# One x tile, not two, through the PE transposes at the start of a gated attention and FFN kernel

## The chip, the cores and the metric

The kernel runs on one core of one Trainium2 chip. The metric is the device time of one execution in microseconds (us), lower is better. PE is the matmul engine (TensorE), PEld its weight loads, DVE is VectorE, ACT is ScalarE, SP is the engine that issues most DMAs, and "SPq" and "ACTq" are the queues on which a DMA is issued.

## The reference, cut to what matters

Two blocks share one input `x` of 2048 tokens by 512 features, in bf16: a linear attention and a gated feed-forward network, mixed by a gate per token.

```python
g = sigmoid((x * gate_w).sum(-1, keepdims=True))
q, k, v = split(x @ wqkv)                 # 32 heads of 16
pq, pk = phi(q), phi(k)                   # phi(t) = (t + 1 if t > 0 else exp(t)) + 1e-6
kv = einsum("bhsd,bhse->bhde", pk, v); z = pk.sum(over tokens)
a = ((pq @ kv) / (pq @ z + 1e-6)) @ wo
b = (silu(x @ w1) * (x @ w3)) @ w2
return g * a + (1 - g) * b
```

## The kernel before

The kernel cuts the tokens into 16 tiles of 128. It needs `x` twice: feature-major (`xT`), as the weights of every matmul that contracts over features, and token-major (`x_sb`), for `XP`, the sum over tokens of `x` times `pk`, from which it gets `kv` later. Tiles 0 and 1 are loaded token-major first and transposed by PE, because those transposes can start before anything else is there. The other tiles come transposed by DMA, and their token-major copies by plain loads later on the same queue.

```python
TF = 2
x_first = x2d[0 : TF * P, :].rearrange("(p j) d -> p j d", j=TF)
dq.dma_start(out=x_sb[:, 0:TF, :], in_=x_first)                      # tiles 0, 1: 256 KB, on SP
nc.scalar.dma_start(out=wk_sb[:, 0:2, :], in_=wqkv_r[:, 0:2, D : 2 * D])   # on ACT
dq.dma_start(out=wk_sb[:, 2:4, :], in_=wqkv_r[:, 2:4, D : 2 * D])
...
dq.dma_start(out=xT[:, :, TF * P : TB], in_=x2d[TF * P : TB, :], transpose=True)   # tiles 2, 3
for tb in range(1, NTB):                                             # four tiles each
    dq.dma_start(out=xT[:, :, tb * TB : (tb + 1) * TB],
                 in_=x2d[tb * TB : (tb + 1) * TB, :], transpose=True)
    x_ts = slice(TF if tb == 1 else tb * TPB, (tb + 1) * TPB)
    dq.dma_start(out=x_sb[:, x_ts, :], in_=x_r[:, x_ts, :])
...  # the other weights follow on the same queue

emit_warm(TB, TB, TB, TB, TB, TB, P, P, P)   # matmuls on constants: keep PE busy until x is there
...
emit_xT(0)                                   # PE transposes, then one copy each on DVE and ACT
emit_xT(1)
for kc, t in ((0, 0), (1, 0), (0, 1), (1, 1), (2, 0), (3, 0)):
    emit_k_mm(k0[t], t, kc)
...  # the rest of k of tiles 0 to 3
for t in range(TPB, NT):                     # from tile 4 on: XP of an earlier tile, then k of tile t
    for u in range(n_xp, n_xp + (2 if t == NT - 4 else 1)):
        emit_xp(u, XP_ps)                    # XP of tile u: needs x_sb of tile u and pk of tile u
        n_xp = u + 1
    emit_k(t)
```

In the timeline below PE runs in the order in which the code emits: XP of tile 0, k of tile 4, XP of tile 1, k of tile 5, and so on.

## Time and profile before

| | before |
|---|---|
| time, median of 3 runs | 179.96 us (179.65 to 180.22) |
| span of the profiled execution | 177.7 us |
| PE busy | 173.0 us, 97% of the span |
| the chain that ended last | 97% PE |

The chain of the page (its part 4) follows the last instruction back to whatever released it, step by step. It is PE almost from end to end, so time can be won or lost only where PE is made to do less, to start earlier or to wait. From the page of the kernel before:

```profile
span 177.7 us, 2453 instructions
PE 173.0 (97%) x868; PEld 83.8 (47%) x884; DVE 117.8 (66%) x203; ACT 65.9 (37%) x124; POOL 63.2 (36%) x71
PE 97%; issue 1%; DVE 0%; DVEq 0%
```

The timeline of the kernel before gives start, length, engine, source line, operation, output and inputs, and the number of merged instructions; a selection of the lines of PE and of the SP queue in the first 12 us:

```profile
0.84 3.04 PE L163 MATMUL warm<-const-bfloat16-1.0 128*128 128x512 bf16 x9 [0.84 <-PEq L473]
1.73 1.32 SPq L89 DMA_TRANSPOSE xT<-in_A_x_dram  x1
3.10 2.81 SPq L93 DMA_TRANSPOSE xT<-in_A_x_dram  x1
3.92 0.89 PE L176 MATMUL xTp<-ident,x_sb 128*128 128x128 bf16 x8
4.70 3.63 PE L186 MATMUL k<-wk_sb,xT 128*128 128x512 bf16 x16
5.96 0.58 SPq L98 DMA_DIRECT2D x_sb<-in_A_x_dram  x1
8.17 1.03 PE L206 MATMUL XP<-pk_sb,x_sb 128*128 128x512 bf16 x4
9.03 1.03 PE L186 MATMUL k_ps<-wk_sb,xT 128*128 128x512 bf16 x4
9.89 1.03 PE L206 MATMUL XP<-pk_sb,x_sb 128*128 128x512 bf16 x4
10.76 1.03 PE L186 MATMUL k_ps<-wk_sb,xT 128*128 128x512 bf16 x4
```

XP of tile 1 is the line at 9.89. PE has no visible gap in these merged lines; the waits view has one wait of 0.3 us, of the first transpose for x. A line on SPq is the time that the issue holds the queue; the data land later. The DMA view of issues that started in a short window gives each landing (the last column is us from issue to landing). For the kernel before, windows around the transposes of tiles 2-3 and 4-7 and the x_sb load behind them:

```profile
xT<-in_A_x_dram SPq DMA_TRANSPOSE x1, 4.5
xT<-in_A_x_dram SPq DMA_TRANSPOSE x1, 4.9
x_sb<-in_A_x_dram SPq DMA_DIRECT2D x1, 768.0 KB, 5.0
```

With the issue times above, tiles 2-3 land at 1.73 + 4.5 = 6.2 us, tiles 4-7 at 8.0, and the token-major tiles 2-7 at 11.0.

### The profile page before, as it was taken

Reading aid. Unit: us, or ns where it says so; the run is one execution under the profiler, and the core shown is the slowest. Engines: PE = TensorE matmul, PEld = TensorE weight load, DVE = VectorE, ACT = ScalarE, POOL = GpSimd, SP = SyncE. Lnnn points to the kernel's source line nnn. Section 1 sums busy time; section 2 is a strip of 40 time slices with the busy share of each in tenths; the row PEclk is TensorE's granted clock in tenths of the full one; section 3 lists DMA queues with packets and bytes.
Section 4 is the critical chain, followed back from the end, with each engine's and each line's share of the span. In section 5 each row is a group of like instructions: output and inputs, shape, how many; then the busy total and the mean of one; then the engine's idle time right before and its main releaser. Section 6 shows DMA issues by size and latency. Waiting matters only on the chain.

```text
span 177.7 us, 2453 instructions
## 1 busy us (share of the span) xinstructions
PE 173.0 (97%) x868; PEld 83.8 (47%) x884; DVE 117.8 (66%) x203; ACT 65.9 (37%) x124; POOL 63.2 (36%) x71
## 2 busy tenths in 40 slices
PE   8999999999999999999999999999999999999993
PEld 3444444474445444444454544444545444444463
DVE  0596858898998637597776466878754668775000
ACT  3624224466433333333244333243434323241211
POOL 5197655967262323262003232710032328000000
PEclk9999999999999999999999999999999999999999
DMA  5999999911014011124000111230002022200011
GB/s 175 234 291 248 300 306 365 348 46 28 9 30 90 6 42 36 38 59 89 0 4 7 40 33 37 71 78 6 0 7 66 7 70 59 59 0 0 30 45 48
DMA packets 30252, 15.14 MB, mean 85 GB/s; under 512 B 20672, under 2 KB 30112, under 8 KB 30240
## 3 DMA queue, kind: packets, MB, share of 16 engines
q1 hardware_dynamic: 29968, 14.72, 30.6%
q10 hardware_dynamic: 272, 0.26, 0.5%
q8 instruction: 7, 0.11, 0.3%
q14 instruction: 5, 0.04, 0.1%
HBM read 8.42 MB, written 2.10 MB: 59 GB/s over the span
## 4 chain that ended last, share of the span: by engine, by line
PE 97%; issue 1%; DVE 0%; DVEq 0%
PE o_ps L357 19%; PE up_ps L320 19%; PE gate_ps L312 19%; PE o_ps L348 8%; PE XP L206 8%; PE q_ps L219 8%; PE k_ps L186 6%; PE r_ps L243 3%; PE k L186 2%; PE o_ps L352 2%; PE warm L163 2%; PE kvT_ps L418 1%; PE xTp L176 0%; PE W_ps L440 0%; PE z_ps L431 0%
## 5 line engine op out<-in xcount | busy, mean ns | idle before, releaser
L312 PE MATMUL gate_ps<-xT,w_sb 128*128 128x512 bf16 x157 | 40.8, 379 | 0.1
L320 PE MATMUL up_ps<-xT,w_sb 128*128 128x512 bf16 x157 | 40.6, 379 | 0.2
L227 POOL TENSOR_TENSOR qz<-pq,z_sb 128x512 f32<-128x512 bf16 x16 | 18.5, 1162 | 59.7 <-DVE pq L147 58.4
L325 ACT ACTIVATE th<-gate_ps 128x512 bf16<-128x512 f32 x40 | 23.9, 597 | 37.9 <-PE gate_ps L312 36.4
L357 PE MATMUL o_ps<-w_sb,hT 128*128 128x512 bf16 (+2 forms) x177 | 37.4, 355 | 0.2
L327 DVE SCALAR_TENSOR_TENSOR gs<-th,gate_ps 128x512 bf16<-128x512 bf16 x40 | 27.3, 682 | 5.6 <-ACT th L325 5.3
L330 DVE TENSOR_TENSOR hT<-up_ps,gs 128x512 bf16<-128x512 f32 x40 | 27.6, 691 | 3.7
L144 DVE TENSOR_SCALAR phi_m<-phi_e 128x512 bf16<-128x512 bf16 x32 | 14.1, 441 | 21.3 <-ACT phi_e L142 21.2
L357 PEld LDWEIGHTS <-hT 128*128 128x128 bf16 x180 | 16.8, 97 | 17.9
L320 PEld LDWEIGHTS <-w_sb 128*128 128x128 bf16 x160 | 15.6, 98 | 18.9
L312 PEld LDWEIGHTS <-w_sb 128*128 128x128 bf16 x160 | 15.6, 98 | 18.7
L362 ACT ACTIVATE o_out<-o_ps,omg 128x512 bf16<-128x512 f32 (+2 forms) x17 | 11.1, 656 | 30.4 <-PE o_ps L357 30.4
L292 POOL TENSOR_TENSOR pqn<-pq,rden 128x512 bf16<-128x512 bf16 x16 | 16.6, 1055 | 14.0 <-DVE rden L285 11.7
L196 POOL TENSOR_TENSOR pks<-pks,pk_sb 128x512 f32<-128x512 f32 x15 | 17.4, 1161 | 7.3 <-DVE pk_sb L147 6.7
L348 PE MATMUL o_ps<-W_sb,pqT 128*128 128x512 bf16 (+2 forms) x70 | 16.7, 355 | 0.1
L230 DVE TENSOR_REDUCE den<-qz 128x32 f32<-128x512 f32 x16 | 10.9, 684 | 8.6 <-POOL qz L227 8.5
L206 PE MATMUL XP<-pk_sb,x_sb 128*128 128x512 bf16 x62 | 16.2, 379 | 0.1
L219 PE MATMUL q_ps<-wq_sb,xT 128*128 128x512 bf16 x61 | 16.1, 380 | 0.1
L142 ACT ACTIVATE phi_e<-k_ps 128x512 bf16<-128x512 f32 x12 | 7.2, 597 | 14.4 <-PE k_ps L186 14.4
L142 ACT ACTIVATE phi_e<-q_ps 128x512 bf16<-128x512 f32 x16 | 9.6, 597 | 7.8 <-PE q_ps L219 6.7
L186 PE MATMUL k_ps<-wk_sb,xT 128*128 128x512 bf16 x48 | 12.3, 379 | 0.0
L147 DVE SCALAR_TENSOR_TENSOR pq<-q_ps,phi_m 128x512 bf16<-128x512 f32 x16 | 11.1, 691 | 0.5
(59 smaller groups left out, 117.3 us busy)
## 6 DMA issues: line engine op xcount, KB each, us to landing
w_sb<-in_B_w_dram SPq DMA_DIRECT2D x6, 640.0 KB, 9.1
out_dram<-o_out SPq DMA_DIRECT2D x15, 128.0 KB, 1.9
x_sb<-in_A_x_dram SPq DMA_DIRECT2D x2, 512.0 KB, 4.2
x_sb<-in_A_x_dram SPq DMA_DIRECT2D x1, 768.0 KB, 5.0
wq_sb<-in_A_wqkv_dram SPq DMA_DIRECT2D x1, 512.0 KB, 5.0
wv_sb<-in_A_wqkv_dram SPq DMA_DIRECT2D x1, 512.0 KB, 6.5
wo_sb<-in_A_wo_dram SPq DMA_DIRECT2D x1, 512.0 KB, 10.4
wk_sb<-in_A_wqkv_dram ACTq DMA_DIRECT2D x1, 256.0 KB, 3.6
```

What stands on the lines that cost most here:

```text
L186: nc.tensor.matmul(k_ps[:], lhsT=xT[:, kc, t * P : (t + 1) * P], rhs=wk_sb[:, kc, :], start=(kc == 0), stop=(kc == KC - 1),)
L196: nc.gpsimd.tensor_add(pks[:], pks[:], pk_sb[:, t, :])
L206: nc.tensor.matmul(XP_ps[dc][:], lhsT=x_sb[:, t, dc * P : (dc + 1) * P], rhs=pk_sb[:, t, :], start=(t == 0), stop=(t == NT - 1),)
L219: nc.tensor.matmul(q_ps[:], lhsT=xT[:, kc, ts_tok], rhs=wq_sb[:, kc, :], start=(kc == 0), stop=(kc == KC - 1),)
L227: nc.gpsimd.tensor_tensor(out=qz[:], in0=st[tb, "pq"][:, tt, :], in1=z_sb[:], op=ALU.mult)
L312: nc.tensor.matmul(gate_ps[:], lhsT=w1_sb[:, kc, fsl], rhs=xT[:, kc, tok_sl], start=(kc == 0), stop=(kc == KC - 1),)
L320: nc.tensor.matmul(up_ps[:], lhsT=w3_sb[:, kc, fsl], rhs=xT[:, kc, tok_sl], start=(kc == 0), stop=(kc == KC - 1),)
L325: nc.scalar.activation(out=th[:], in_=gate_ps[:], func=ACT.Tanh, scale=0.5)
L327: nc.vector.scalar_tensor_tensor(out=gs[:], in0=th[:], scalar=1.0, in1=gate_ps[:], op0=ALU.add, op1=ALU.mult)
L330: nc.vector.tensor_tensor(out=st[tb, "hT"][:, fc, :], in0=up_ps[:], in1=gs[:], op=ALU.mult)
L348: nc.tensor.matmul(o_ps[:], lhsT=st[tb, "pqT"][:, c, tsl], rhs=W_sb[:, c, a:b], start=(c == 0), stop=False,)
L357: nc.tensor.matmul(o_ps[:], lhsT=st[tb, "hT"][:, fc, tsl], rhs=w2_sb[:, fc, a:b], start=False, stop=(fc == FC - 1),)
```

## The change

The intent: only tile 0 goes through PE, so the first load is half as large, PE transposes half as much and k can start earlier. Tile 1 now comes transposed by its own small DMA, behind `wk`, and its token-major copy comes with those of tiles 2 and 3, behind the transpose of tiles 4-7. The cut diff:

```diff
-    TF = 2
-    x_first = x2d[0 : TF * P, :].rearrange("(p j) d -> p j d", j=TF)
-    dq.dma_start(out=x_sb[:, 0:TF, :], in_=x_first)
+    dq.dma_start(out=x_sb[:, 0, :], in_=x_r[:, 0, :])
 ...
-    dq.dma_start(
-        out=xT[:, :, TF * P : TB], in_=x2d[TF * P : TB, :], transpose=True
-    )
+    for a, b in ((P, 2 * P), (2 * P, TB)):
+        dq.dma_start(out=xT[:, :, a:b], in_=x2d[a:b, :], transpose=True)
     for tb in range(1, NTB):
         ...  # the transpose of four tiles
-        x_ts = slice(TF if tb == 1 else tb * TPB, (tb + 1) * TPB)
-        dq.dma_start(out=x_sb[:, x_ts, :], in_=x_r[:, x_ts, :])
+        if tb == 1:
+            dq.dma_start(out=x_sb[:, 1:TPB, :], in_=x_r[:, 1:TPB, :])
+        if tb < NTB - 1:
+            x_ts = slice(tb * TPB, NT if tb == NTB - 2 else (tb + 1) * TPB)
+            dq.dma_start(out=x_sb[:, x_ts, :], in_=x_r[:, x_ts, :])
 ...  # w2 in one load in place of two; outputs of tiles 0 and 1 in plain rows
-    emit_warm(TB, TB, TB, TB, TB, TB, P, P, P)
+    emit_warm(TB, TB, TB, TB, TB, P, P)
 ...
     emit_xT(0)
-    emit_xT(1)
-    ...  # k of tiles 0 and 1 interleaved
+    emit_warm(TB)
+    ...  # k of tiles 0 to 3 in order
```

## The prediction

> **What bounds the kernel.** TensorE. On the page of before PE is busy 173.0 of 177.7 us (97%), and the chain that ended last is 97% PE. In the timeline PE runs without a visible gap from 0.84 us: nine warm-ups to 3.88, eight transposes 3.92 to 4.81, k of tiles 0-3 to 8.33, then XP and k in turn, 0.86 us each. So only what shortens or delays PE in the first 12 us can move the time. Weights have slack: wq lands at 20.7 us (first used at 29.9), the first w1 half at about 27 (used at 38.2).
>
> **What the change does.**
> - Removes four PE transposes (eight took 0.89 us, so about 0.45) and their two copies.
> - One 512-wide warm-up (0.43 us start to start) and one 128-wide fewer before the transposes, one 512-wide behind them, to cover the copy.
> - x tile 0 is 128 KB in place of 256 KB. The 256 KB landed at 3.91 us and PE waited 0.3 us for it (waits view). At 300 to 340 GB/s half should land near 3.3.
> - Tile 1 (128 rows) becomes a DMA transpose. From 4.5 to 7.4 us the first two transposes moved 768 rows, 3.8 ns each: 128 rows cost about 0.48 us, the plain 128 KB they replace about 0.35.
>
> **Critical path after.** Estimates from before's landings: PE transposes 3.3-3.8, k of tile 0 from about 4.2, at first at the slow rate; the second half of wk (5.27 before) near 4.9, so k0 ends near 5.3. Tile 1's transpose lands near 5.4, that of tiles 2-3 near 6.35 (6.23 before), that of tiles 4-7 near 8.1 (8.0). So k of tile 2 begins near 6.35 against 6.5: the start is now held by DMA transposes, and of a possible 0.45 us only 0.1 to 0.2 is kept. Then the new risk: tile 1's token-major rows, in SBUF from the start before, now arrive in a 384 KB load issued behind the transpose of tiles 4-7, near 6.6 us. The 768 KB load in that place was issued at 5.96, moved its first bytes only at about 8.2 and landed at 10.96. I expect this one at 9.9 to 10.5. XP of tile 1 is due at about 9.8 (9.89 before). So PE stalls there by 0.1 to 0.7 us, and the gain is given back.
>
> Later loads move little; the transpose of tiles 12-15, behind a 1 MB load now, lands at 18 to 20 us instead of 17.0, and is used at 22.8. The single w2 load, the output rows and the tail change nothing.
>
> The Trainium skill ("TensorE: Matmul & The Clock Gate", Part 1) says PE runs at half rate until about 3.4 us of activity; this trace agrees, 0.43 us per 512-wide matmul until about 4.5 us, then 0.215. I expect the switch at the same time.
>
> **Prediction.** 180.1 us, 8 in 10 between 179.4 and 180.9. Faster by over 2%: 0.01; within 2%: 0.98; slower by over 2%: 0.01.
>
> **What the profile would show.** Right: k starts near 4.2 us; small waits on DMA for xT before tile 1 or 2; a wait on the x_sb load before XP of tile 1; from 13 us on the same timeline with a constant shift under 0.6 us. Wrong: XP of tile 1 follows k of tile 4 without wait (then up to 0.5 us lower), or k of tile 4, 8 or 12 waits for its transpose.
>
> **What would make it wrong.** Transposes slower or later than rows times 3.8 ns; a gap in early PE work that keeps the slow clock longer; the x_sb load starting as soon as it is issued.

## The result, and the profile after

| | before | after |
|---|---|---|
| time, median of 6 runs | 179.63 us (179.28 to 180.22) | 180.22 us (179.90 to 180.50) |
| ratio, with 95% interval | 1 | 1.0029 (1.0007 to 1.0051) |
| span of the profiled execution | 177.7 us | 178.7 us |

A ratio is the mean time of one kernel's fast runs over that of the other's of the same rounds, so it is not quite the ratio of the medians. By the 2% rule the two are the same; the interval says slightly slower. The change made the start earlier and the time longer, and the question is where the gain went. The timeline of the kernel after, same lines:

```profile
0.84 2.51 PE L160 MATMUL warm<-const-bfloat16-1.0 128*128 128x512 bf16 x7 [0.84 <-PEq L468]
1.73 2.63 SPq L87 DMA_TRANSPOSE xT<-in_A_x_dram  x2
3.44 0.60 PE L173 MATMUL xTp<-ident,x_sb 128*128 128x128 bf16 x4
4.27 4.95 PE L183 MATMUL k<-wk_sb,xT 128*128 128x512 bf16 x16
4.40 2.01 SPq L89 DMA_TRANSPOSE xT<-in_A_x_dram  x1
6.40 0.15 PEld L183 LDWEIGHTS <-xT 128*128 128x128 bf16 x1 [0.28 <-issue]
6.45 0.58 SPq L94 DMA_DIRECT2D x_sb<-in_A_x_dram  x1
9.06 1.03 PE L203 MATMUL XP<-pk_sb,x_sb 128*128 128x512 bf16 x4
9.92 1.03 PE L183 MATMUL k_ps<-wk_sb,xT 128*128 128x512 bf16 x4
10.95 0.55 PEld L203 LDWEIGHTS <-x_sb 128*128 128x128 bf16 x4 [0.50 <-DMA x_sb<-in_A_x_dram]
10.95 1.04 PE L203 MATMUL XP<-pk_sb,x_sb 128*128 128x512 bf16 x4
11.82 1.03 PE L183 MATMUL k_ps<-wk_sb,xT 128*128 128x512 bf16 x4
```

And the landings of the kernel after, in the DMA view: tiles 2-3, tiles 4-7, then the x_sb load of tiles 1-3:

```profile
xT<-in_A_x_dram SPq DMA_TRANSPOSE x1, 3.5
xT<-in_A_x_dram SPq DMA_TRANSPOSE x1, 4.8
x_sb<-in_A_x_dram SPq DMA_DIRECT2D x1, 384.0 KB, 4.5
```

Three things are to be seen.

1. k begins at 4.27 in place of 4.70 us: the start won 0.43 us, as intended.
2. The first 16 matmuls of k took 4.95 in place of 3.63 us. There is no gap in them; PE ran at half rate longer. (Most weight loads take 0.15 us at half rate and 0.10 at full rate; the one at 6.40 above is among the last of 0.15 in this trace, and the very last starts at 6.83 us, in that of before at 4.43.)
3. XP of tile 1 starts at 10.95 in place of 9.89 us, and the weight load in front of it waited for the x_sb load, which landed at 6.45 + 4.5, about 10.9. By the starts of its matmuls PE itself lost only 0.17 us there, since it came late; but with a landing at 10.9 an earlier PE would have had to wait until then too. The two transposes at 1.73 hold the queue 2.63 us where one held it 1.32, so the transpose of tiles 4-7 is issued at 4.40 in place of 3.10. It holds the queue for less time than before, 2.01 in place of 2.81 us, so its issue ends 0.5 us later, not 1.3; it lands at 9.2 in place of 8.0. The smaller x_sb load behind it lands as late as the larger one did before.

From here on nothing differs. The chain of waits has k of tile 5 start at these times in the two kernels (start, length, what), before and then after:

```profile
10.92 0.86 PE k_ps L186 x4
```

```profile
11.99 0.86 PE k_ps L183 x4
```

The span less this start is 177.7 - 10.9 = 166.7 us before and 178.7 - 12.0 = 166.7 us after. So "when does k of tile 5 start" is a ruler for everything below. It gave a remainder between 166.7 and 166.9 us in every profile of an ordinary execution in which I could read it.

Points 2 and 3 are two candidate causes, and in this one trace they overlap. That made the theories. **A**: the late x_sb load of tiles 1-3 sets the time, and the moment of the clock switch is chance. **B**: the changed warm-up made PE leave its half rate later. **C**, on why the loads are late: a DMA transpose of 128 rows holds the queue as long as one of 256.

### The profile page after: what moved, and what is told of

Same layout as the page of the kernel before. It is cut to its first block, busy times and chain, and to the rows that moved or that the text cites. A ratio compares the mean times of both kernels' runs of the same rounds, so it can differ in the third digit from the quotient of the medians.

```text
span 178.7 us, 2441 instructions
## 1 busy us (share of the span) xinstructions
PE 174.0 (97%) x863; PEld 83.7 (47%) x879; DVE 119.0 (67%) x202; ACT 65.7 (37%) x123; POOL 63.1 (35%) x71
## 4 chain that ended last, share of the span: by engine, by line
PE 96%; DMA 1%; issue 1%; DVE 0%; DVEq 0%
PE gate_ps L309 19%; PE o_ps L354 19%; PE up_ps L317 19%; PE q_ps L216 8%; PE o_ps L345 8%; PE XP L203 8%; PE k_ps L183 6%; PE r_ps L240 3%; PE k L183 3%; PE o_ps L349 2%; DMA x_sb<-in_A_x_dram 1%; PE kvT_ps L413 1%; PE W_ps L435 0%; PE xTp L173 0%; PE warm L160 0%
## 5 line engine op out<-in xcount | busy, mean ns | idle before, releaser
L354 PE MATMUL o_ps<-w_sb,hT 128*128 128x512 bf16 (+2 forms) x176 | 36.8, 355 | 0.2
L141 DVE TENSOR_SCALAR phi_m<-phi_e 128x512 bf16<-128x512 bf16 x32 | 15.4, 482 | 22.2 <-ACT phi_e L139 22.1
L183 PE MATMUL k_ps<-wk_sb,xT 128*128 128x512 bf16 x47 | 12.3, 379 | 0.1
```

The source lines that it names most:

```text
L183: nc.tensor.matmul(k_ps[:], lhsT=xT[:, kc, t * P : (t + 1) * P], rhs=wk_sb[:, kc, :], start=(kc == 0), stop=(kc == KC - 1),)
L354: nc.tensor.matmul(o_ps[:], lhsT=st[tb, "hT"][:, fc, tsl], rhs=w2_sb[:, fc, a:b], start=False, stop=(fc == FC - 1),)
```

## The experiments

Each kernel is the kernel before or after with one edit, or with two (e10). All gave the correct output. Three groups were each run on one chip beside the same runs of before: e1 to e4, then e5 to e8, then e5b, e9 and e10; the medians of before were 179.89, 179.87 and 179.70 us.

### Both kernels once more, and two ways to move the wait (e1 to e4)

e1_before_again and e2_after_again have no edit.

> The unchanged kernel before, once more: the noise floor and the clock. Theory A (the late x_sb load of tiles 1-3 sets the time of the changed kernel; when PE leaves its half rate is a matter of chance): time equal to before within 0.3%, and the last half-rate weight load may fall anywhere from 4.2 to 7.7 us, not again at 4.43. Theory B (the changed warm-up made PE leave its half rate at 6.8 in place of 4.4 us, and that is the loss): the switch is again within 0.3 us of 4.4.

> The changed kernel, once more. Theory A: XP of tile 1 starts again within 0.2 us of 10.95, right behind the landing of the x_sb load of tiles 1-3, even if the clock switches at another moment; ratio to before about 1.003 again. Theory B: the switch is again near 6.8, and XP of tile 1 moves with it.

Measured, five rounds: e1 179.83 us, ratio 0.9997 (0.9969 to 1.0026); e2 180.37 us (180.06 to 181.2), ratio 1.0034 (1.0008 to 1.0059). The loss repeats. But the switch did not: the last half-rate weight load is at 5.03 us in e1 and at 3.68 us in e2, earlier than in either trace of before. Theory B is out as worded: the same kernel gave 6.83 and 3.68. A shift of a few tenths in the mean moment is not excluded: over all ordinary profiles here the last half-rate load lies between 3.15 and 5.47 us in the five with nine warm-ups in a row and between 3.68 and 6.83 in the seven with the changed warm-up. Yet with the clock on its side the profiled execution of e2 took 180.06 us, still above the median of before, 179.89. Its timeline says why:

```profile
4.16 0.60 PE L183 MATMUL k<-wk_sb,xT 128*128 128x512 bf16 x2
4.96 1.63 PE L183 MATMUL k<-wk_sb,xT 128*128 128x512 bf16 x6 [0.19 <-DMA wk_sb<-in_A_wqkv_dram]
7.06 1.90 PE L183 MATMUL k<-wk_sb,xT 128*128 128x512 bf16 x8 [0.47 <-DMA xT<-in_A_x_dram]
10.41 0.64 PEld L203 LDWEIGHTS <-x_sb 128*128 128x128 bf16 x4 [0.22 <-DMA x_sb<-in_A_x_dram]
10.52 1.03 PE L203 MATMUL XP<-pk_sb,x_sb 128*128 128x512 bf16 x4
11.38 1.03 PE L183 MATMUL k_ps<-wk_sb,xT 128*128 128x512 bf16 x4
```

A fast PE waited for the second half of wk and then for the transpose of tiles 2-3, which landed at 7.0 us here (6.2 before). XP of tile 1 started at 10.52, so my expectation of 10.95 within 0.2 missed, and its weight load waited only 0.2 us for x_sb, which landed at 10.4; PE itself lost nothing there. So theory A names one of two late landings, and where PE is fast the other comes first.

e3_lag changes PE's order alone:

```diff
-        for u in range(n_xp, n_xp + (2 if t == NT - 4 else 1)):
+        for u in range(n_xp, n_xp + {TPB + 1: 0, NT - 4: 2, NT - 3: 2}.get(t, 1)):
```

> Only PE's order changes: k of tile 5 runs before XP of tile 1, so the late x_sb load has one more 0.86 us slot; every load is issued as in the changed kernel. Theory A: no wait for x_sb before XP of tile 1; the time falls against the changed kernel by 0.2 us (clock switch near 6.8) to 0.9 us (switch near 4.4), so about 0.5 us in the mean, to a ratio to before of 0.999 to 1.001. Theory B: the order of PE does not touch the clock, so the time stays at 1.003 of before, less at most 0.17 us.

Measured: 179.93 us, ratio 1.0005 (0.9983 to 1.0027). Every run (179.86 to 180.01) is below every run of e2. Its timeline shows k of tiles 4 and 5 in one piece, then XP of tile 1 with no wait:

```profile
4.29 4.62 PE L183 MATMUL k<-wk_sb,xT 128*128 128x512 bf16 x16
8.74 1.03 PE L203 MATMUL XP<-pk_sb,x_sb 128*128 128x512 bf16 x4
9.60 1.89 PE L183 MATMUL k_ps<-wk_sb,xT 128*128 128x512 bf16 x8
11.33 1.03 PE L203 MATMUL XP<-pk_sb,x_sb 128*128 128x512 bf16 x4
```

The load landed at 10.8 us, just before it was wanted. Moving that use by one slot takes the loss away, 0.44 us between the medians, inside the 0.2 to 0.9 that A named and above the 0.17 that B allowed. The edit puts XP of every later tile a slot back as well, until near the end; but in neither trace of the changed kernel did PE wait for a load after XP of tile 1, so that use is the one that can matter. The traces do not show the size: the idle time of PE at XP of tile 1 was 0.17 us in the one and nothing in the other, and the traced executions of e2 and e3_lag, 180.06 and 180.01 us, are 0.05 apart. The 0.44 comes mostly from executions that were not traced, and what PE waited for in them is inferred.

e4_swap moves the load ahead of the transpose of tiles 4-7:

```diff
+    dq.dma_start(out=x_sb[:, 1:TPB, :], in_=x_r[:, 1:TPB, :])
     for tb in range(1, NTB):
         ...  # transpose of four tiles
-        if tb == 1:
-            dq.dma_start(out=x_sb[:, 1:TPB, :], in_=x_r[:, 1:TPB, :])
```

> Only the queue's order changes: the x_sb load of tiles 1-3 goes ahead of the transpose of tiles 4-7. Theory A: the load lands near 7.5 to 8 us, XP of tile 1 does not wait for it; instead the transpose of tiles 4-7 lands near 10 (9.17 before) and k of tile 4 may wait for it up to 0.7 us. Time below the changed kernel by 0.1 to 0.6 us. Theory B: no difference beyond 0.17 us.

Measured: 180.88 us, ratio 1.0056 (1.0031 to 1.0080): the fall that I expected did not come. The median is 0.5 us above that of e2, though the intervals of the two overlap. The load landed at 8.0 us as expected, and XP of tile 1 no longer waited for it. But the transpose of tiles 4-7 landed at 9.9, and in the chain of waits k of tile 4 stands behind it:

```profile
5.02 4.89 DMA xT<-in_A_x_dram
9.91 0.05 issue
9.96 1.04 PE k_ps L182 x4
```

The queue has no spare time there: a load moved forward pushes the next one back into PE's way. I had named this wait, but had weighed it too lightly.

### Why the loads are late (e5, e6, e9), and two other cures (e7, e8)

e5_split is the kernel before with its transpose of tiles 2-3 cut into two of 128 rows; e5b_split_again is the same kernel.

```diff
-    dq.dma_start(out=xT[:, :, TF * P : TB], in_=x2d[TF * P : TB, :], transpose=True)
+    for a, b in ((TF * P, 3 * P), (3 * P, TB)):
+        dq.dma_start(out=xT[:, :, a:b], in_=x2d[a:b, :], transpose=True)
```

> The kernel before, with its one DMA transpose of tiles 2-3 (256 rows, 1.32 us on the queue) cut into two of 128 rows; nothing else. Theory C (issuing a DMA transpose of 128 rows takes as long on the queue as one of 256, about 1.3 us, so the changed kernel's extra one pushed all later loads back by that): the transpose of tiles 4-7 is issued near 4.4 us in place of 3.10 and lands at 8.7 to 9.2 in place of 7.96, the x_sb load of 768 KB lands at 11.3 to 11.9 in place of 10.93; k of tile 4 waits up to 0.2 us, XP of tile 2 up to 0.3, less where the clock switches late; time equal to before to 0.3 us more. Rival, cost by rows (each half takes about 0.65 us): issue of tiles 4-7 stays at about 3.1 to 3.2 and nothing moves.

> The same kernel as e5_split, whose only profiled execution was a freak one of 478 us with PE at well under its usual rate. Theory C: transpose of tiles 4-7 issued near 4.4 us (3.10 in before), landing at 8.5 to 9.2 (7.96), x_sb load of 768 KB landing at 11.3 to 11.9 (10.93); k of tile 5 starts at 11.0 to 11.6 (10.92 in before, 11.05 in its repeat), time 0 to 0.5 us over before. No execution far over 181 us again.

Measured: e5 180.27 us, ratio of its fast runs 1.0017 (0.9993 to 1.0042). Its profiled execution was a freak of 478.27 us, counted as slow: PE was busy 467.2 us, a 512-wide matmul of the FFN took 839 ns in the mean (379 before). The granted clock of 1.0 that is listed for it is no measurement: this trace holds no clock record, and the tool then gives 1.0. The other five runs were 179.42 to 180.5. e5b, three rounds: 180.1 us (179.78 to 181.24), ratio 1.0037 (1.0007 to 1.0066), with a normal profile. Its timeline of the SP queue:

```profile
1.73 2.58 SPq L90 DMA_TRANSPOSE xT<-in_A_x_dram  x2
4.35 1.95 SPq L92 DMA_TRANSPOSE xT<-in_A_x_dram  x1
6.35 0.58 SPq L97 DMA_DIRECT2D x_sb<-in_A_x_dram  x1
```

Theory C holds: the two halves took 2.58 us where the whole took 1.32, the transpose of tiles 4-7 was issued at 4.35 in place of 3.10 and landed at 8.5 in place of 8.0, and the 768 KB load landed at 11.5 in place of 11.0. One cut did all that, with the same bytes. As in the kernel after, the issue of tiles 4-7 was shorter (1.95 us, 2.81 before), so it ended only 0.4 us later, which fits a landing 0.5 us later. In this kernel the use of that load is one tile later, so PE did not wait: k of tile 5 starts at 11.45, late only because the switch fell at 5.5 us. Whether the cut itself costs time the runs do not settle; one of e5b's four runs is a 181.24.

e9_units, one look, cut other transposes of the kernel before, as a ruler:

```diff
+        for a, n in {1: ((0, 256), (256, 256)), 2: ((0, 512),), 3: ((0, 128), (128, 384))}[tb]:
+            lo = tb * TB + a
+            dq.dma_start(out=xT[:, :, lo : lo + n], in_=x2d[lo : lo + n, :], transpose=True)
```

> A ruler: the kernel before with its later DMA transposes cut differently: tiles 4-7 as two of 256 rows, tiles 12-15 as one of 128 and one of 384. If a transpose takes about 1.3 us on the queue per started 256 rows: 1.3 each for the two, 1.3 for 128, 2.4 to 2.6 for 384, and the sum for tiles 4-7 is as before (2.8). If there is a fixed cost of about 1 us per transpose, whatever its rows: the two of 256 rows take no less than the one of 512 plus 1 us, 3.8 in all. Loads full of earlier work may lengthen the later ones. No more than 0.3 us of time either way.

Measured, in a single run: 180.24 us (against a median of 179.70, above the 0.3 us that I allowed). The two of 256 rows held the queue 1.96 and 1.31 us, that of 128 rows 1.19, that of 384 rows 2.34. So 128 rows cost what 256 do, and 384 cost a second step; 3.3 us for the pair is more than the 2.8 expected by steps and less than the 3.8 of a fixed cost, but its first issue may have been held by the loads in flight. The x_sb load landed at 12.3 us, and XP of tile 2 waited for it.

e6_merge is the kernel after with tiles 1 to 3 in one transpose of 384 rows:

```diff
-    for a, b in ((P, 2 * P), (2 * P, TB)):
+    for a, b in ((P, TB),):
```

> The changed kernel, with the transposes of tile 1 and tiles 2-3 in one DMA of 384 rows. Theory C: about 2 us of issue in place of 2.6, so that of tiles 4-7 is issued near 3.8 (4.40), and lands near 8.4; the x_sb load lands near 10.2 (10.4 to 10.9). In return k of tile 1 waits for the joined transpose until about 6.4 (5.5), which with an early clock switch costs up to 1 us of PE's start. Time within 0.3 us of the changed kernel. Rival, cost by rows: issue of tiles 4-7 stays at 4.4.

Measured: 180.59 us, ratio 1.0046 (1.0027 to 1.0066). The issue took 2.41 us, so the next came at 4.18 in place of 4.40, less than expected; the x_sb load landed at 10.1. The chain shows the wait that this bought:

```profile
1.73 4.80 DMA xT<-in_A_x_dram
6.53 0.05 issue
6.57 2.76 PE k L183 x12
```

k of tile 1 starts at 6.57, so nothing is left of the early start.

e8_early1 is the kernel after with the token-major copy of tile 1 loaded early on the other queue:

```diff
+    nc.scalar.dma_start(out=x_sb[:, 1, :], in_=x_r[:, 1, :])
     dq.dma_start(out=wk_sb[:, 2:4, :], in_=wqkv_r[:, 2:4, D : 2 * D])
 ...
-            dq.dma_start(out=x_sb[:, 1:TPB, :], in_=x_r[:, 1:TPB, :])
+            dq.dma_start(out=x_sb[:, 2:TPB, :], in_=x_r[:, 2:TPB, :])
```

> The changed kernel, with the token-major copy of tile 1 (128 KB) loaded early, second on the ScalarE queue; tiles 2-3 stay where they were. Theory A: it lands before 5 us, XP of tile 1 follows k of tile 4 without a wait, the time falls by 0.2 to 0.6 us against the changed kernel, to about what the reordered PE gave (179.9). What is left over before is then the transposes: tiles 4-7 land at 9 to 9.5 us in place of 7.96. If the x_sb load is not the cause: time as the changed kernel or, by 128 KB more in front of the transposes, 0.3 us more.

Measured: 179.89 us, ratio 1.0009 (0.9988 to 1.0029). XP of tile 1 did not wait, and in the median the loss is gone as with e3_lag. This is weaker evidence: the changed kernel was not run in this group, its two intervals (1.0007 to 1.0051 and 1.0008 to 1.0059) overlap this one, and two of the six runs, the traced one among them, took 180.3. The price of the early load is in the timeline of that run:

```profile
4.00 0.97 PE L184 MATMUL k<-wk_sb,xT 128*128 128x512 bf16 x2
5.52 3.67 PE L184 MATMUL k<-wk_sb,xT 128*128 128x512 bf16 x14 [0.56 <-DMA wk_sb<-in_A_wqkv_dram]
```

k waited 0.56 us for the second half of wk, which landed at 5.5 (4.9 after), and tiles 2-3 landed at 7.2 (6.6). The small load itself landed at 5.7, later than the 5 that I expected. The Trainium skill ("DMA: Bandwidth & Descriptors", section "Issuing engines are not separate DMA queues") says that DMAs from different engines run on the same 16 DMA engines and interleave. This run agrees: 128 KB on the ACT queue delayed the SP queue's next loads by about 0.6 us against the trace of the kernel after.

e7_pe1 is the kernel before with the small first load, but tile 1 still transposed by PE:

```diff
-    x_first = x2d[0 : TF * P, :].rearrange("(p j) d -> p j d", j=TF)
-    dq.dma_start(out=x_sb[:, 0:TF, :], in_=x_first)
+    for t in range(TF):
+        dq.dma_start(out=x_sb[:, t, :], in_=x_r[:, t, :])
...  # outputs of tiles 0 and 1 in plain rows
-    emit_warm(TB, TB, TB, TB, TB, TB, P, P, P)
+    emit_warm(TB, TB, TB, TB, TB, P, P, P, P)
```

> The part of the change that starts PE early, without the DMA transpose of tile 1: x tiles 0 and 1 come as two plain loads of 128 KB, both transposed by PE as before, five wide and four narrow warm-ups, everything else as before. Theory A with C: first PE transpose near 3.45 us as in the changed kernel (3.92 before), k of tile 0 near 4.45 (4.70 before), held by the first half of wk; no wait for xT or x_sb of tiles 1-3; time 0.1 to 0.4 us below before (ratio 0.998 to 0.9995), so 0.5 to 0.9 below the changed kernel. If the start of k does not reach the end (rival): equal to before.

Measured: 180.0 us (179.78 to 181.71), ratio 1.0031 (0.9997 to 1.0065): no gain, against my expectation. The chain names the step that failed:

```profile
1.27 3.34 DMA x_sb<-in_A_x_dram
4.61 0.05 issue
4.66 0.40 PE xTp L175 x4
5.05 3.47 PE k L185 x16
```

Tile 0 landed at 3.5 us, but tile 1, as a load of its own, only at 4.6, where one load of both had landed at 3.9. So k starts at 5.05 in this chain, and at 4.81 in that of before. Why the second of two small loads is so much later was not tested.

### Both cures at once (e10)

e10_lag_early is e8_early1 with the PE order of e3_lag, both edits as shown.

> The changed kernel with both cures at once: PE's order of e3_lag and the early copy of tile 1 of e8_early1. If both took away the same wait (theory A), they do not add up: 179.8 to 180.0, as each alone, now held by the transposes of tiles 2-3 and 4-7 (k of tile 2 starts behind a landing at 6.6 to 7.2 us, 6.21 in before) and, with a late switch, by the clock. If they took away different waits: 0.3 us or more below each alone.

Measured: 179.95 us, ratio 1.0021 (1.0001 to 1.0041). The cures do not add up, as is to be expected if they removed the same wait. But the runs prove little: in this group before had 179.70, so this kernel is 0.25 us above it, its interval just leaves out 1, and it overlaps those of the changed kernel too. The chain of this run:

```profile
1.73 4.27 DMA xT<-in_A_x_dram
6.05 2.76 PE k L184 x12
```

With the x_sb wait gone, k of tile 1 stands behind its own DMA transpose, which landed at 6.0 us (I had named tile 2). No kernel tried here beats the one before.

## Why the prediction was right or wrong

The predicted time, 180.1 us, and its range hold: 180.22 us. That it is so near is luck: 180.1 was 0.1 us above the 179.96 then known of before, the measured loss is 0.5 us (0.29%), and the two meet only because the six runs of before came out at 179.63. The central step, that PE would lose the gain at XP of tile 1 to the late token-major load, is borne out by e3_lag: with PE's order alone changed, every run is below every run of the changed kernel beside it, and the kernel is level with before (1.0005). e8_early1 points the same way (1.0009) with less certainty, and e10, with both cures, is not clearly level (1.0021). Point by point:

- *"k of tile 0 from about 4.2", tile 0 landing "near 3.3"*: right. 4.27 us and 0.81 + 2.6 = 3.4 us.
- *"128 rows cost about 0.48 us"*: this step failed. I took a transpose's cost as rows times 3.8 ns, from the rate at which data moved. Measured by what it holds the queue, that transpose cost 1.28 us, as long as the 1.32 of 256 rows (e5b_split_again shows the same for a cut alone). So tiles 4-7 were issued 1.3 us later (their issue ended 0.5 and 0.8 us later) and landed at 9.2 and 8.8 us in the two traces, where I expected 8.1 (8.0 before). The cut alone accounts for about 0.5 us of that, its effect in e5b_split_again; the rest came together with the 128 more rows to transpose and was not tested apart.
- *Tiles 2-3 "near 6.35"*: 6.6 and 7.0 in the two traces. "The start is now held by DMA transposes" was right in kind. With an early switch (e2_after_again) PE waited for them, and the 0.1 to 0.2 us that I thought would be kept was lost.
- *The x_sb load at "9.9 to 10.5"*: 10.9 and 10.4. It was issued at 6.45 and 6.76, near 6.6 as expected; it came late because what stands before it in the queue did (put ahead of the transpose of tiles 4-7, in e4_swap, it landed at 8.0). The skill ("DMA: Bandwidth & Descriptors", section "Queues, rings and completion order") says that each DMA engine consumes a queue's descriptors in ring order; the order of the landings here agrees (3.4, 4.9, 5.5, 6.6, 9.2 and 10.9 us for the first six on SP after), though the section adds that completion need not keep that order.
- *"PE stalls there by 0.1 to 0.7 us"*: right in place, and by luck in size. PE's own idle time there was below 0.2 us, because PE came late itself: through its half rate in one trace, through the wait for tiles 2-3 in the other. What counts is that XP of tile 1 started at 10.95 and 10.52, against 9.89.
- *"I expect the switch at the same time"*: wrong. The skill ("TensorE: Matmul & The Clock Gate", Part 1) says that the activity window is free-running and 3.4 us long, so that the switch depends on where in it the kernel starts. I had used the length and ignored the phase. In the twelve profiles of ordinary executions the last half-rate weight load falls between 3.15 and 6.83 us, which begins below the 4.2 us that I named in the expectation of e1. For the same kernel it was 4.43 and 5.03 (before), 6.83 and 3.68 (after). One trace against one trace would have told a false story here.
- *Later loads, the single w2 load and the tail change nothing*: right; 166.7 us remain after k of tile 5 starts, in both.

What stays open: how long PE waited for x_sb in the executions that were not traced, since the idle time seen in the two traces (0.17 us and none) is less than the 0.5 us lost; what share of the remaining time is held by the clock and what by the transposes once the x_sb wait is gone. e3_lag's six runs lie within 0.15 us while those of before spread over 1.1 us; I have no test of why.

## What to carry to other kernels

Starting an engine 0.4 us earlier is worth only what the loads behind it can follow: list the landing of each next operand, and when two uses follow in turn, ask which of them can be put one slot later, which cost nothing that e3_lag could measure, before moving loads in a full queue. Cost a DMA by what it holds the queue as well as by its bytes, since one more issue in front delayed the loads behind it (by 0.5 to 0.8 us in e5b_split_again). And before blaming a difference between two traces, profile each kernel twice: what differs between two traces of the same kernel is no effect of the change.

## What the Trainium skill lacked or had wrong

- "DMA: Bandwidth & Descriptors" gives no issue time by rows for DMA transposes from HBM on this chip (its one figure for "previous generations", 631 sequencer cycles for small tiles, names no rows). Here 128 rows of 512 bf16 held the queue 1.19 to 1.29 us, 256 rows 1.29 to 1.32 us (1.96 once, with loads in flight), 384 rows 2.34 to 2.41 us. The time is no function of the rows alone: the 512 rows of tiles 4-7 took 2.81 us in before and 1.95 in e5b_split_again, behind one more issue.
- "TensorE: Matmul & The Clock Gate", Part 1, gives the switch to full rate as about 4 us into matmul activity, varying by 500 ns from run to run. With PE busy from 0.84 us, the last half-rate weight load fell between 3.15 and 6.83 us in twelve profiles of ordinary executions. The free-running window of 3.4 us on the same page fits that spread; the 500 ns do not. The page's own note further down, of 6, 11 or 14 slow matmuls for one kernel, is nearer to it. Ten of the twelve traces also hold a clock record: full clock begins between 3.50 and 6.23 us and lasts 174.08 us in each, 51 windows of the page's 3413 ns. The earliest, in e7_pe1, comes 2.7 us after PE's first matmul, sooner than the page's first 3.4 us at half rate.
- The same page mentions a clock seen stuck low for more than 50 us. One execution here ran 478 us, with 512-wide FFN matmuls at 839 ns in place of 379. In its chain four 512-wide matmuls take 2.35 or 2.48 us from end to end of the run, about 0.6 us each against 0.43 at half rate. Its trace holds no clock record, so what held PE back is not known.
- No page says how far apart two small loads issued back to back on one queue land beside a load on another: 128 KB each, issued 0.46 us apart, landed 1.1 us apart (3.5 and 4.6 us), one load of both at 3.9.
